# Linear attention and a gated MLP on one core: the spatial product of three batches in a 2x2 block form of seven products, denominators inverted on few columns, and another rule for the order

## The chip, the cores and the metric

The kernel runs on one core of one Trainium2 chip. The metric is the time of one execution in device microseconds (us), as the median of several runs. Less is better. Engines are called by their names in the profile: PE is TensorE (matmuls; PEld its loads of the stationary operand), DVE is VectorE, ACT is ScalarE, POOL is GpSimd, and SP (SyncE) issues nearly all DMAs.

## The reference

Linear attention over four batches of four heads (1088 positions, 32 columns a head) gives x of 1088 x 128 for each batch. It goes through an MLP whose gate mixes the positions:

```python
kv  = einsum('bhsf,bhsd->bhfd', phi(k), v)           # phi: 64 products a_i*b_j of two 8-wide projections
den = einsum('bhsf,bhf->bhs', phi(q), sum_s phi(k)) + 1e-6
x   = einsum('bhsf,bhfd->bhsd', phi(q), kv) / den    # heads side by side: (4, 1088, 128)

h    = gelu(x @ w_in)                # 128 -> 1024
u, v = h[..., :512], h[..., 512:]
v_n  = (v - mean(v)) / sqrt(var(v) + 1e-6) * g_ln
v_s  = einsum('ts,bsd->btd', w_sg, v_n) + b_sg       # w_sg: 1088 x 1088, the spatial product
out  = x + (u * v_s) @ w_out         # 512 -> 128
```

All values are fp32.

## The kernel before

**Numbers in two words.** TensorE multiplies fp32r words. Each fp32 operand is split into a high word and a low word (a cast on ACT, a subtraction on DVE), and a product takes three matmuls: high by high, low by high, high by low.

**The spatial product.** The 1088 positions that are summed over make nine row tiles t, eight of 128 rows and a last one of 64. The last needs two matmuls, since its tile holds the high words in its upper and the low words in its lower half. The 512 columns of v make four column blocks (db), the 1088 result positions three chunks (ci) of 364, 362 and 362 (376, 376 and 336 in the last batch). A unit (db, ci) is 3 matmuls into `pu` (L395 to L397, the u half of `w_in`), 26 into `pz` (L378: vh by w_h, L380: vl by w_h, L386: vh by w_l) and 3 into `po` (L463 to L465, by `w_out`). Here `w_h` and `w_l` hold the high and low words of `w_sg`, transposed, for the whole run, and `vh`, `vl` those of one column block of the normalized v (L363, L368, L371).

**Around a unit.** ACT takes `pu` through the gelu (L400). DVE moves `pz` out of its bank, scaled by `g_col` with `b_bc` added (L407), multiplies by u (L430), and with ACT's cast splits the result into `gh`, `gl` (L433, L434). After the fourth block of a chunk DVE adds x (L473, L474), and SP stores the result (L475).

**The next batch meanwhile.** While batch b is swept, attention of batch b+1 is made as side work: k projections (L189 PE, L192 ACT, L148 DVE), the sum kv (L204), q projections (L231 splits q, L237 to L239), and the features of q. These go by way of DRAM: `ab` is written to `e_0d` and its like repeated (L158, L163), read back as two operands of 128 rows (L169), multiplied (L248), and split (L250 on ACT, L251 on POOL). L261 to L263 give numerator and denominator together. ACT puts the denominators, each repeated over its head's 32 rows, into `den` (L267), DVE inverts all 128 rows (L270) and multiplies (L274), and x is split (L278, L280). Then come v (L299 to L301), gelu (L305), mean and variance, the inverse root by small operations on DVE (L320 to L345), and the normalized v (L350).

**The order.** A head, with a table of its own (`HEAD`), loads and splits the weights (the low words of w at L951) and makes attention of batch 0. Then every batch's units go in a loop, and `Plan` puts the side work between them at ticks from two tables, `FIRST` for batch 1 and `LATER` for 2 and 3. A scheduler below gives the evacuations of a unit priority (`AHEAD`). SP issues its DMAs in program order; when one waits, those behind it wait too.

## Time and profile before

| | |
|---|---|
| time, median of 3 runs (lowest, highest) | 358.16 us (357.82, 358.75) |
| span of the profiled execution, first to last instruction | 356.8 us |
| granted TensorE clock, mean | 0.997 |
| PE, DVE, ACT, POOL busy | 348.4, 233.5, 186.2, 22.1 us |
| DMA traffic | 30.19 MB, 28.1% of 16 engines' span in SP's queue |
| instructions | 5497 |

The profiled execution's own time is its span and what lies around it; the median of the three runs is 1.4 us above that span. In a group's row stand the line, engine and operation, the result and operands, shapes and count, then busy us, mean ns of one, and the idle time of the engine just ahead of the group with what ended it. A row of a timeline starts with the start and the duration in us. A row of waits has the total, the count and the longest. A row by windows gives for each stretch the busy time and count of each engine, the granted clock, the share of the DMA engines and GB/s. A DMA row ends with KB of one and the us from issue to landing.

### The profile page before, as it was taken

How to read it: one execution, taken by the hardware profiler on the slowest of the kernel's cores; microseconds unless marked ns; L12 is line 12 of the kernel's file. 1: busy time of each engine (PE TensorE's matmuls, PEld its weight loads, DVE VectorE, ACT ScalarE, POOL GpSimd, SP SyncE). 2: the span in 40 equal slices, each digit the busy share in tenths (PEclk: the TensorE clock that was granted, in tenths of full speed). 3: DMA queues.
4: the chain of work that ended last, by engine and by line, in shares of the span. 5: the costliest groups of instructions: out<-in, count | busy, mean ns of one | idle time of the engine just before them, and what ended most of it. 6: DMA issues, size and time to landing. Idle time of an engine off the chain costs nothing.

```text
span 356.8 us, 5497 instructions
## 1 busy us (share of the span) xinstructions
PE 348.4 (98%) x2024; PEld 323.1 (91%) x2024; DVE 233.5 (65%) x552; ACT 186.2 (52%) x463; POOL 22.1 (6%) x37
## 2 busy tenths in 40 slices
PE   8999999999999999999999999999999999999995
PEld 7875669898999989999898999999998999999994
DVE  4797899987929359636846766654867656552333
ACT  5475951346394983314558992323368992132120
POOL 0003000131020000022020000021120000000000
PEclk9999999999999999999999999999999999999998
DMA  7993001959200032883000006671000000100001
GB/s 228 396 410 136 2 0 31 215 153 250 71 0 2 1 83 87 224 226 121 2 0 21 3 21 147 189 177 54 0 2 1 2 0 24 42 0 2 0 2 62
DMA packets 18266, 30.19 MB, mean 85 GB/s; under 512 B 1984, under 2 KB 15168, under 8 KB 18240
## 3 DMA queue, kind: packets, MB, share of 16 engines
q1 hardware_dynamic: 18096, 29.76, 28.1%
q8 instruction: 16, 0.26, 0.3%
q10 hardware_dynamic: 144, 0.09, 0.1%
q14 instruction: 10, 0.08, 0.1%
HBM read 20.92 MB, written 8.91 MB: 84 GB/s over the span
## 4 chain that ended last, share of the span: by engine, by line
PE 88%; DVE 5%; ACT 3%; POOL 1%; issue 1%; DMA 1%; DVEq 0%; ACTq 0%
PE pz L378 19%; PE pz L386 19%; PE pz L380 17%; PE pkv L204 3%; PE pu L395 2%; PE pz L937 2%; PE po L465 2%; PE pu L397 2%; PE pu L396 2%; PE po L463 2%; PE po L464 2%; PE pv L299 2%; PE pab L813 2%; PE pk L189 2%; PE pv L300 2%; PE pv L301 2%
## 5 line engine op out<-in xcount | busy, mean ns | idle before, releaser
L378 PE MATMUL pz<-w_h,vh 128*128 128x362 f32 (+3 forms) x405 | 133.7, 332 | 0.0
L386 PE MATMUL pz<-w_l,vh 128*128 128x362 f32 (+3 forms) x405 | 129.4, 329 | 0.0
L380 PE MATMUL pz<-w_h,vl 128*128 128x364 f32 (+3 forms) x360 | 118.1, 328 | 0.0
L378 PEld LDWEIGHTS pz<-w_h,vh 128*128 128x128 f32 x405 | 75.7, 188 | 1.5 <-DVE gt L407 0.6
L386 PEld LDWEIGHTS pz<-w_l,vh 128*128 128x128 f32 x405 | 75.6, 188 | 0.3
L380 PEld LDWEIGHTS pz<-w_h,vl 128*128 128x128 f32 x360 | 67.8, 188 | 0.8
L433 ACT CAST gh<-gt 128x362 fp32r<-128x362 f32 (+3 forms) x47 | 23.1, 495 | 59.0 <-PE po L464 50.5
L407 DVE SCALAR_TENSOR_TENSOR gt<-pz,g_col,b_bc 128x362 f32<-128x362 f32 (+3 forms) x47 | 27.7, 592 | 39.9 <-PE pz L386 39.4
L434 DVE TENSOR_TENSOR gl<-gt,gh 128x362 fp32r<-128x362 f32 (+3 forms) x47 | 24.8, 531 | 15.1 <-ACT gh L433 14.9
L400 ACT ACTIVATE u<-pu 128x362 f32<-128x362 f32 (+3 forms) x48 | 22.4, 471 | 18.1 <-PE pu L397 15.4
L430 DVE TENSOR_TENSOR gt<-gt,u 128x362 f32<-128x362 f32 (+3 forms) x47 | 25.0, 532 | 8.1 <-ACT u L400 7.5
L350 ACT ACTIVATE vn<-vn,nm,rs 128x512 f32<-128x512 f32 x36 | 27.7, 811 | 4.7 <-POOL nm L684 3.9
L270 DVE RECIPROCAL den<-den 128x362 f32<-128x362 f32 (+1 forms) x9 | 21.8, 2418 | 10.0 <-ACT den L267 10.0
L368 DVE TENSOR_TENSOR vl<-vn,vh 128x384 fp32r<-128x384 f32 (+2 forms) x60 | 22.9, 420 | 7.5 <-ACT vh L363 7.3
L363 ACT CAST vh<-vn 128x384 fp32r<-128x384 f32 (+1 forms) x63 | 23.1, 420 | 3.4 <-PE pz L386 3.4
L308 ACT ACTIVATE waste<-vn,mv 128x512 bf16<-128x512 f32 x27 | 19.6, 726 | 0.3
L305 ACT ACTIVATE vn<-pv 128x512 f32<-128x512 f32 x27 | 16.0, 595 | 6.4 <-PE pv L301 6.3
L937 PE MATMUL pz<-w_f,vn 128*128 128x362 f32 (+3 forms) x54 | 18.0, 476 | 0.8 <-ACT vn L350 0.7
L395 PE MATMUL pu<-x_h,win_h 128*128 128x362 f32 (+3 forms) x48 | 16.7, 349 | 0.0
L937 PEld LDWEIGHTS pz<-w_f,vn 128*128 128x128 f32 (+1 forms) x54 | 9.8, 189 | 7.6 <-ACT vn L350 2.4
L463 PE MATMUL po<-gh,wout_h 128*128 128x362 f32 (+3 forms) x47 | 16.0, 341 | 0.0
L396 PE MATMUL pu<-x_h,win_l 128*128 128x362 f32 (+3 forms) x48 | 15.7, 328 | 0.0
(201 smaller groups left out, 530.6 us busy)
## 6 DMA issues: line engine op xcount, KB each, us to landing
w_f<-in_w SPq DMA_DIRECT2D x9, 544.0 KB, 9.8
vx<-in_v SPq DMA_DIRECT2D x8, 288.0 KB, 6.6
k<-in_k SPq DMA_DIRECT2D x3, 576.0 KB, 4.2
e_0d<-ab SPq DMA_DIRECT2D x3, 364.0 KB, 4.0
e_0d<-ab SPq DMA_DIRECT2D x6, 182.0 KB, 5.3
e_0a<-e_0d SPq DMA_DIRECT2D x3, 364.0 KB, 4.7
e_0b<-e_0d SPq DMA_DIRECT2D x3, 364.0 KB, 4.6
q<-in_q SPq DMA_DIRECT2D x6, 181.0 KB, 2.4
```

What stands on the lines that cost most here:

```text
L350: A.activation(self.vn[:, t], self.vn[:, t], AF.Identity, bias=self.nm[:, t : t + 1], scale=self.rs[:, t : t + 1])
L363: A.copy(vh[:, ts], vs[:, ts])
L378: last = mm(z, lhsT=vh[:, t], rhs=w_h[:, t, cs], start=(t == 0), stop=False)
L380: last = mm(z, lhsT=vl[:, t], rhs=w_h[:, t, cs], start=False, stop=False)
L386: mm(z, lhsT=self.parts[db][0][:, t], rhs=w_l[t][:, c0 : c0 + cw], start=False, stop=(t == NT - 1))
L395: mm(pu, lhsT=win_h[:, ws], rhs=xh[:, cs], start=True, stop=False)
L407: V.scalar_tensor_tensor(gt, z, g_col[:, db : db + 1], b_bc[:, c0 : c0 + cw], op0=ALU.mult, op1=ALU.add)
L430: V.tensor_mul(gt, gt, u)
L433: A.copy(gh, gt)
L434: V.tensor_sub(gl, gt, f32(gh))
L463: mm(o, lhsT=wout_h[:, db], rhs=gh, start=(db == 0), stop=False)
L937: return mm(zs[ci], lhsT=g.vn[r, t, :P], rhs=w_f[t][r, c0 : c0 + cw], start=(t == 0), stop=(t == NT - 1),)
```

## The change

**Seven products.** In batches 1 to 3 two column blocks (A1 = 2p, A2 = 2p + 1) are worked together. Over the result chunks 0 and 1, now of 362 columns each, and the row tiles 0 to 3 and 4 to 7, the product is a 2x2 block product. `pair` does it in seven block products of 4 row tiles x 3 matmuls, where eight were done before. Four operands are sums of blocks of v, made and split on DVE and ACT by 512 columns (`words`); four operands of w are its own blocks, and the others are sums of blocks. The last 64 rows (`tail`) and chunk 2, of 364 columns (`whole`), stay as they were. A pair has nine evacuations (`evac`, L859) instead of six: three of them add onto an earlier result, and some take the negated `ng_col`. Batch 0 keeps the plain product.

**Sums of w.** `combine` makes them once, while batch 0 is swept, from reloaded pieces of w: DVE and ACT build and split them, and SP writes them to DRAM as t1, t2, t3, beside a copy tb of the block that stood there; a fourth stays on chip (`t4a`, `t4b`). `stream` then loads one of them into columns 362 to 723 of `w_h` and `w_l`, four row tiles and two words a time, so that the same place holds another operand for the next product: streams 1, b, 2 and 3 in each pair (1 and b alone in the very last).

**Denominators.** One row of each head's denominators is written to DRAM as 4 x 364, read back as 112 x 13, inverted there (L1081), written back, and read as 128 rows, four rows repeated 32 times (L1079 to L1083); then comes the multiplication (L1084).

**Features of q.** `ab` goes to DRAM once (L1051). One operand is read with repeated rows (L1053), the other by `spread` (L792), eight loads of 16 rows.

**Smaller moves.** The subtraction that was L251 on POOL is on DVE (L1062). The small operations of the norm go from DVE to POOL. The low words of w (L739) leave the head's table and are made in the new order.

**The order.** `Plan` is now a list scheduler over all the work behind the head: each instruction has an engine, a duration, and what it reads and writes; PE's main work is in its given sequence, the side work has fractions of a batch in `SIDE`, and `DELAY` holds back the `po` matmuls.

The diff, cut to its core:

```diff
-CH = [(0, 364), (364, 362), (726, 362)]
+CH = [(0, 362), (362, 362), (724, 364)]
+CA = [(0, 364), (364, 364), (728, 360)]
+CD = [13, 13, 12]
+HW = 181
...
-FIRST = [
-    -15.472, 20.135, 12.008, 13.876, 14.942, 31.02, 18.196, 16.249, 11.271, 38.899, 15.025, 30.832, 23.931,
...
+DELAY = 5.83
+SIDE = [
+    dict(k=(0, 0.0241), q=(0.065, 0.0107), n=(0.0314, 0.1822), v=(0.6703, 0.0732)),
...
-            G.tensor_sub(qpl, a, f32(qph))
...
-            V.reciprocal(den, den)
...
+    def spread(e, d):
+        for i in range(R):
+            last = load(e[16 * i : 16 * i + 16], d)
+        return last
...
+    def group(z, zk, cw, e, t, w, wk, first, last):
+        def f():
+            o, (wh, wl) = z()[:, :cw], w()
+            mm(o, lhsT=ar[e][:, 0, t], rhs=wh, start=first, stop=False, skip_group_check=True)
+            mm(o, lhsT=ar[e][:, 1, t], rhs=wh, start=False, stop=False, skip_group_check=True)
+            mm(o, lhsT=ar[e][:, 0, t], rhs=wl, start=False, stop=last, skip_group_check=True)
...
+    def stream(n, half):
+        for t in range(4):
+            add("SP", dma(370), lambda t=t: [load(f32(w_h[:, t + half, 362:724]), td[n][t, 0]), load(f32(w_l[t + half][:, 362:724]), td[n][t, 1])],
+                r=[("td", n, t)], w=[("w", t + half, 1)])
...
+            add("SP", 0.08, lambda cw=cw, ci=ci: load(dd[ci][0, :, :cw], now["r2"][0:P:32, :cw]), r=[("r", 2, 0), ("r", 2, 1)], w=[("dd", ci)])
+            add("SP", 0.08, lambda cw=cw, ci=ci, n=n, dr=dr: load(dr, dd[ci][0, :, :cw].rearrange("h (i n) -> h i n", n=n)), r=[("dd", ci)], w=["dr"])
+            add("V", 0.5, lambda dr=dr: [V.tensor_scalar(dr, dr, EPS, None, op0=ALU.add), V.reciprocal(dr, dr)], w=["dr"])
...
+            add("SP", dma(190), lambda cw=cw, ci=ci: load(now["r4"][:, :cw], dd[ci][1, :, :cw].unsqueeze(1).broadcast_to([H, 32, cw])), r=[("dd", ci)], w=[("r", 4)])
...
+        add("V", dv(512), lambda: V.tensor_add(a[0, 0], a[0, 0], a[1, 0]), r=ak[1, 0], w=ak[0, 0])
+        add("V", dv(512), lambda: V.tensor_add(sg, a[0, 0], a[1, 1]), r=ak[0, 0] + ak[1, 1], w=gk)
+        words(ar[e[2]], lambda: sg, ("ar", e[2]), gk)
+        words(ar[e[3]], lambda: a[0, 0], ("ar", e[3]), ak[0, 0])
...
+        unit(b, ca)
+        product(X, xk, e[0], (0, 0), True)
+        evac(b, c11, X, xk, g_col)
+        whole(Z, zk, 2, e, 0)
...
+        product(X, xk, e[2], (0, 1), False)
+        stream("1", 0)
...
+        product(X, xk, e[3], (4, 1), False)
+        stream("b", 4)
...
+        product(Z, zk, e[0], (0, 1), True, (1, 1))
+        if more:
+            stream("2", 0)
...
+        product(X, xk, e[2], "t4", False, (0, 2))
...
+        product(Z, zk, e[1], (4, 1), False, (1, 3))
+        if more:
+            stream("3", 4)
```

**Where instructions stand.** First PE in the sweep of batch 1. Before, early in the sweep of a batch, two units stand side by side (`pz_0_0` and `pz_0_1` are the accumulators of block 0, chunks 0 and 1; `pu`, `po` and `pab` those of the u half, of the result and of the q projection):

```order
L397 MATMUL pu_0_1_2393<-x_l,win_h 128x362
L378 MATMUL pz_0_1_2399<-w_h,vh_0_2099 128x362
L380 MATMUL pz_0_1_2399<-w_h,vl_0_2100 128x362
L386 MATMUL pz_0_1_2399<-w_l_525,vh_0_2099 128x362
L378 MATMUL pz_0_1_2399<-w_h,vh_0_2099 128x362
L380 MATMUL pz_0_1_2399<-w_h,vl_0_2100 128x362
L386 MATMUL pz_0_1_2399<-w_l_573,vh_0_2099 128x362
L463 MATMUL po_0_1838<-gh_3_0_2214,wout_h 128x364
L237 MATMUL pab_0_2406<-qt_0h,sk_h 128x364
L378 MATMUL pz_0_0_2327<-w_h,vh_0_2099 128x364
L238 MATMUL pab_0_2406<-qt_0h,sk_l 128x364
L380 MATMUL pz_0_0_2327<-w_h,vl_0_2100 128x364
```

In the changed kernel, in the first pair of batch 1 (`w_l_636` is row tile 0 of w's low words, `t4a` the sum kept on chip, `ar_92` and `ar_94` operands of v, `bz_608` and `bz_609` the two accumulators, each with one of the seven products):

```order
L927 MATMUL bz_609<-w_h,ar_94 128x362
L928 MATMUL bz_609<-w_h,ar_94 128x362
L929 MATMUL bz_609<-w_l_636,ar_94 128x362
L881 MATMUL po_0_1817<-gh_602,wout_h 128x362
L882 MATMUL po_0_1817<-gh_602,wout_l 128x362
L883 MATMUL po_0_1817<-gl_604,wout_h 128x362
L843 MATMUL bs_607<-x_h,win_h 128x364
L844 MATMUL bs_607<-x_h,win_l 128x364
L845 MATMUL bs_607<-x_l,win_h 128x364
L927 MATMUL bz_608<-t4a,ar_92 128x362
L928 MATMUL bz_608<-t4a,ar_92 128x362
L929 MATMUL bz_608<-t4a,ar_92 128x362
```

Row tiles of two products stand interleaved: behind the first row tile of the product that reads stream 1, other units and the product by the sum on chip are put before its second row tile.

SP about the passage from batch 0 to batch 1. Before, loads for batch 2 (`in_k`, `in_v`, `in_q`) and the repetition of the features (`e_2d` of one batch, then `e_0d` of the next, from `ab`):

```order
L181 DMA k_2107<-in_k 128x1152
L169 DMA e_2b<-e_2d 128x2x362
L185 DMA vx<-in_v 128x576 x2
L225 DMA q_0_2353<-in_q 128x364
L225 DMA q_1_2359<-in_q 128x362
L225 DMA q_2_2536<-in_q 128x362
L158 DMA e_0d<-ab_0_2410 256x1x364
L163 DMA e_0d<-ab_0_2410 16x8x364 x2
```

In the changed kernel, in the first pair of batch 1 (`t_613` is t1, `t_614` and `t_615` the other two sums, `dq_618` the features on their way, x8 eight loads in a row):

```order
L996 DMA w_l_715<-t_614 128x362
L1051 DMA dq_618<-ab 64x364
L1080 DMA dr_124<-dd_620 112x13
L1039 DMA qld<-in_q 128x364
L996 DMA w_h<-t_613 128x362
L996 DMA w_l_636<-t_613 128x362
L1053 DMA e_1751<-dq_618 128x1x364
L792 DMA e_1759<-dq_618 16x364 x8
L1053 DMA e_1776<-dq_618 128x1x364
L792 DMA e_1784<-dq_618 16x364 x8
L996 DMA w_h<-t_613 128x362
L996 DMA w_l_656<-t_613 128x362
```

Between row tile 0 (`w_l_636`) and row tile 1 (`w_l_656`) of stream 1 there are 18 loads of features. In the first pair of batch 2 the same loads stand within stream b, and the way back of the denominators stands ahead of it:

```order
L1051 DMA dq_618<-ab 64x364
L1082 DMA dd_620<-dr_124 112x13
L900 DMA out<-gt_597 128x362
L996 DMA w_h<-tb 128x362
L996 DMA w_l_760<-tb 128x362
L996 DMA w_h<-tb 128x362
L996 DMA w_l_774<-tb 128x362
L1053 DMA e_2666<-dq_618 128x1x364
L792 DMA e_2673<-dq_618 16x364 x8
L1053 DMA e_2685<-dq_618 128x1x364
L792 DMA e_2690<-dq_618 16x364 x8
L996 DMA w_h<-tb 128x362
```

Here tiles 4 and 5 of b are ahead of the features and tiles 6 and 7 behind them.

More of the change, by code (lines that the diff above doesn't have):

```diff
@@ L77, in f32, with f32r @@
     return ap.bitcast(F32)
+def f32r(ap):
+    return ap.bitcast(F32R)
 class Pool:
@@ L1046, in tile_kernel @@
-    for b in range(B):
-        first, extra = (1, start()) if b == 0 else (0, [])
-        if b + 1 < B:
-            s = Side(b + 1, (NB - first) * 27)
-            with ExitStack() as stack:
-                if b == 0:
-                    for ins in head.last:
-                        stack.enter_context(tc.issue_after(ins))
-                g.main(late, s.tick, first, pend, extra)
-                s.plan.run()
-            g = s.g
-        else:
-            g.end(NB - 1, len(CH) - 1)
-            g.main(late, lambda: None, first, pend)
@@ new lines, in slot, with area @@
+    def slot(b, p):
+        return p * (1 + b % 2)
+    def area(b, db, half):
+        s, sub = slot(b, db // 2), db % 2
+        c = 256 * s + P * sub
+        if half == 2:
+            return vn[:, 8, c : c + P]
+        return vn[:, 4 * half : 4 * half + 4, c : c + P]
+    for c in range(3):
+        add(None, 0, None, w=[("po", c)], start=START["PE"])
+    for t in range(NT):
+        lo = add("V", 1.29, head.s.steps["wlo", t][2], w=[("w", t, c) for c in range(3)], after=[lo] if t else [])
@@ new lines, in tile_kernel, with pemain, unit @@
+    done_lo = lo
+    clock = [0.0]
+    def pemain(dur, f, d=0.0, **kw):
+        i = add("PE", dur, f, pos=clock[0] + d, **kw)
+        if d == 0.0:
+            clock[0] += dur
+        return i
+    nout = {}
+    def unit(b, q, d=0.0):
+        db, ci = q
+        c0, cw = CH[ci]
+        k = ("pu", b, q)
+        xh, xl = xs[b % 2]
+        def f():
+            o, cs, ws = ps(k)[:, :cw], slice(c0, c0 + cw), slice(P * db, P * db + P)
+            mm(o, lhsT=win_h[:, ws], rhs=xh[:, cs], start=True, stop=False)
+            mm(o, lhsT=win_l[:, ws], rhs=xh[:, cs], start=False, stop=False)
+            mm(o, lhsT=win_h[:, ws], rhs=xl[:, cs], start=False, stop=True)
+        pemain(3 * pe(cw), f, d, r=[("win",)] + [("x", b % 2, c) for c in range(3)], take={k: "ps"})
+        u = ("u", b, q)
+        add("A", 0.05 + ac(cw), lambda: A.activation(utt[plan.got[u]][:, :cw], ps(k)[:, :cw], AF.Gelu_apprx_tanh),
+            r=[k], take={u: "u"}, free=[k])
@@ new lines, in product @@
+    def product(z, zk, e, where, first, more=None):
+        for t in range(4):
+            if where == "t4":
+                w, wk = (lambda t=t: t4(t)), ("t4", t)
+            else:
+                w, wk = (lambda t=t: wsel(t + where[0], where[1])), ("w", t + where[0], where[1])
+            group(z, zk, HW * 2, e, t, w, wk, first and t == 0, t == 3 and more is None)
+        if more:
+            tail(z, zk, *more)
+    td = {n: dram.tile([4, 2, P, HW * 2], F32, name="t" + n) for n in ("1", "2", "3", "b")}
@@ new lines, in tile_kernel, with at, standard @@
+    dq = [dram.tile([64, CW], F32, name=f"dq{i}") for i in range(3)]
+    dd = [dram.tile([2, H, CW], F32, name=f"dd{i}") for i in range(3)]
+    def at(b, kind, i):
+        a, d = SIDE[b - 1][kind]
+        return starts[b - 1] + (a + d * i) * LONG[b - 1]
+    starts, LONG = [0.0], (104.0 - 8, 70.0, 70.0, 58.0)
+    for n in LONG:
+        starts.append(starts[-1] + n)
+    def standard(b, db, ci, zi, e, i):
+        zk = ("psn", zi)
+        unit(b, (db, ci))
+        whole(lambda: pzt[zi], zk, ci, e, i)
+        evac(b, (db, ci), lambda: pzt[zi], zk, g_col)
+        gate(b, (db, ci), DELAY)
@@ new lines, in tile_kernel @@
+    for ci in range(3):
+        evac(0, (1, ci), zs[ci], zks[ci], g_col, free=["z12"] if ci == 2 else ())
+        if ci:
+            unit(0, (1, ci))
+        gate(0, (1, ci), DELAY)
+    attention(1)
+    for ci in (0, 1, 2):
+        standard(0, 2, ci, ci % 2, (2, 3), 1)
+        if ci == 0:
+            for h in range(2):
+                split(0, 3, h, h)
+            rest(0, 3, 2)
+            combine()
+    for n, ci in enumerate((1, 0, 2)):
+        standard(0, 3, ci, (n + 1) % 2, (0, 1), 2)
+        if ci == 1:
+            stream("2", 0)
+            stream("3", 4)
@@ L1064 @@
+    zi, e = 0, (2, 3, 0, 1)
+    for b in range(1, B):
+        clock[0] = starts[b]
+        if b == B - 1:
+            before_end(b)
+        pair(b, 0, e, zi)
+        if b + 1 < B:
+            attention(b + 1)
+        pair(b, 1, e, 1 - zi)
+    with tc.manual_schedule():
+        plan.run(START, START["PE"])
 def kernel(q, k, v, S1, S2, moe_w_in, moe_g_ln, moe_w_sg, moe_b_sg, moe_w_out):
```

1019 lines of the change are left out of this document (570 added, 449 removed), and 11 rows, old and new, of tables (FIRST, LATER).

## The prediction

> **What bounds the kernel now.** I read the page first: busy times, the clock by slices, the chain of waits.
>
> ```profile
> PE 348.4 (98%) x2024; PEld 323.1 (91%) x2024; DVE 233.5 (65%) x552; ACT 186.2 (52%) x463; POOL 22.1 (6%) x37
> PEclk9999999999999999999999999999999999999998
> PE 88%; DVE 5%; ACT 3%; POOL 1%; issue 1%; DMA 1%; DVEq 0%; ACTq 0%
> ```
>
> TensorE is busy for 98% of the span at full clock, and holds 88% of the chain that ended last. A busy time of pipelined matmuls counts overlaps, so the price of one is read from the timeline, as the distance between starts. This is the first of 23 spatial matmuls in a row, and the matmul behind them:
>
> ```profile
> 199.69 0.33 PE L380 MATMUL pz<-w_h,vl 128*128 128x362 f32 x1
> ...
> 203.52 0.32 PE L463 MATMUL po<-gh,wout_h 128*128 128x362 f32 x1
> ```
>
> (203.52 − 199.69) / 23 = 0.1665 us for one matmul of 362 columns. Then the engines by stage (the head, then the sweeps of batches 0 to 3, each cut at the first unit of its batch), and who TensorE waited for:
>
> ```profile
> 0.00:51.00 51.00, 48.77 (x242) 35.11 (x242) 39.73 (x123) 33.46 (x60) 3.60 (x18) 1.00 0.55 205
> 51.00:120.00 69.00, 68.06 (x402) 64.29 (x402) 53.94 (x101) 35.05 (x97) 7.08 (x7) 1.00 0.35 93
> 120.00:204.00 84.00, 82.96 (x492) 78.79 (x492) 54.15 (x133) 49.87 (x134) 5.70 (x6) 1.00 0.30 82
> 204.00:286.00 82.00, 82.00 (x497) 79.42 (x496) 53.69 (x126) 46.68 (x125) 5.71 (x6) 1.00 0.26 64
> 286.00:357.00 71.00, 66.60 (x398) 65.50 (x396) 31.95 (x72) 21.16 (x49) 0.00 (x0) 0.98 0.05 17
> PE pk L189 <- ACT u L400: 1.1, 2, 0.8
> PE warm L144 <- POOL vx L124: 0.9, 1, 0.9
> PE pz L937 <- ACT vn L350: 0.7, 2, 0.5
> ...
> PE pnd L852 <- DVE qp L820: 0.2, 1, 0.2
> ```
>
> From 51 us on TensorE has almost no hole, and its waits, eight rows of which the first three and the last stand here, come to 4.0 us in all. So each matmul taken out counts in full, and each wait put in does too. VectorE (columns: PE, PEld, DVE, ACT, POOL, clock, DMA share, GB/s) uses 54 us of 82 to 84 in batches 1 and 2, but 54 of 69 in batch 0; the DMA engines a third or less.
>
> **Part 1, the matmuls.** A pair of column blocks took 6 x 26 = 156 spatial matmuls. Now seven products of 4 row tiles x 3 matmuls make 84, four ends of column groups on the last 64 rows 8, the two chunks left whole 52: 144. Six pairs save 72 x 0.1665 = **−12.0 us**. The order of the instructions has just these counts, so this term is sure, apart from the pitch. The Trainium skill (TensorE: Matmul & The Clock Gate, Back-to-back issue gap) gives N/2.4 + 2.5 ns for a lone warm stream, 153 ns at 362 columns, by which the saving would be 11.0 us; the trace has 166.5, and the measurement decides.
>
> **Part 2, rewriting w in place.** The product needs three sums of w's blocks beside the block itself in the same columns, so SP writes them over one another: four streams a pair of eight loads of 185 KB, 192 loads. What a DMA costs on SP and until it lands:
>
> ```profile
> 86.55 0.37 SPq L169 DMA_DIRECT2D e_2b<-e_2d  x1
> 87.02 0.41 SPq L185 DMA_DIRECT2D vx<-in_v  x1
> 87.52 0.38 SPq L225 DMA_DIRECT2D q<-in_q  x1
> out<-o SPq DMA_DIRECT2D x6, 181.0 KB, 2.2
> e_0d<-ab SPq DMA_DIRECT2D x6, 182.0 KB, 5.3
> GB/s 228 396 410 136 2 0 31 215 153 250 71 0 2 1 83 87 224 226 121 2 0 21 3 21 147 189 177 54 0 2 1 2 0 24 42 0 2 0 2 62
> ```
>
> An issue holds SP 0.37 to 0.41 us, back to back 0.47 to 0.50; I take 0.42. Landing of 181 KB is 2.2 us at best, 5.3 us when the queue is full. A stream's first load may go once the last matmul on that row tile has read, and has to land before the next product reads it. In the order of the changed kernel that leaves, over the twelve streams that are read next (streams 1 and b; 2 and 3 have over 140 matmuls of time), 33 matmuls in the first pair of batch 1 and 41 to 62 in the others: 41 x 0.1665 = 6.8 us or more. A stream alone needs 8 x 0.42 = 3.4 us of SP and 2.2 us of landing; its fourth row tile comes free 9 matmuls = 1.5 us after the first, so it takes 4.1 us, and at the best rate of the GB/s row (1.48 MB at 410 GB/s) 3.6 + 2.2 − 1.5 = 4.3 us. Hidden, with some 2.5 us to spare.
>
> Two streams are broken up on SP. In the first pair of batch 1 the loads of row tile 1 of stream 1 stand behind 18 loads of the q features (two e loads, sixteen 16-row spreads). They land 2 x 0.42 + 18 x 0.42 + 2 x 0.42 + 2.2 = 11.4 us after tile 0 came free; TensorE wants them 43 matmuls later, 7.2 us: **+4.3 us**. In the first pair of batch 2 another 18 stand within stream b; 18 x 0.42 + 4 x 0.42 + 2.2 = 11.4 us against 62 matmuls, 10.3 us: **+1 us**. Both ends: nothing, if a 23 KB issue is much cheaper than any row of this trace, and 5 us more if they land in 5.3 us. No row has a 16-row load; the nearest, a 2 KB load of g_col, held SP like the large ones, so I take 0.42.
>
> ```profile
> 13.05 0.33 SPq L839 DMA_DIRECT2D g_col<-in_g  x1
> ```
>
> The Trainium skill (DMA: Bandwidth & Descriptors, Rules for kernel authors) says to coalesce small transfers and calls those under 64 KB mostly overhead; the 144 spreads are such. Another section of that page, Issuing engines are not separate DMA queues, calls the sequencer's time to initiate a DMA usually small beside the DMA itself; by that the 5.3 us would be near nothing.
>
> **Part 3, work on VectorE and ScalarE.** What the added and removed work costs:
>
> ```profile
> L407 DVE SCALAR_TENSOR_TENSOR gt<-pz,g_col,b_bc 128x362 f32<-128x362 f32 x24 | 14.1, 593 | 16.5 <-PE pz L386 16.3
> L659 DVE TENSOR_TENSOR win_l<-wi0t,wi0e 128x512 fp32r<-128x512 f32 x1 | 0.7, 694 | 0.0
> L434 DVE TENSOR_TENSOR gl<-gt,gh 128x362 fp32r<-128x362 f32 x24 | 12.7, 530 | 1.3 <-ACT gh L433 1.2
> L270 DVE RECIPROCAL den<-den 128x362 f32<-128x362 f32 x6 | 14.5, 2416 | 8.2 <-ACT den L267 8.2
> L951 DVE TENSOR_TENSOR w_l<-w_f,w_h 128x1088 fp32r<-128x1088 f32 x8 | 10.3, 1283 | 0.0
> 107.39 0.53 DVE L434 TENSOR_TENSOR gl<-gt,gh 128x362 fp32r<-128x362 f32 x1
> 107.83 0.53 DVE L430 TENSOR_TENSOR gt<-gt,u 128x364 f32<-128x364 f32 x1
> 108.32 2.42 DVE L270 RECIPROCAL den<-den 128x362 f32<-128x362 f32 x1
> L368 DVE TENSOR_TENSOR vl<-vn,vh 128x128 fp32r<-128x128 f32 x24 | 5.9, 288 | 7.4 <-ACT vh L363 7.3
> L330 DVE TENSOR_TENSOR h<-h,ve 128x5 f32<-128x5 f32 x1 | 0.2, 168 | 0.0
> L684 POOL TENSOR_TENSOR nm<-np,rs 128x3 f32<-128x3 f32 x1 | 0.7, 659 | 0.1
> ```
>
> A swept batch gains 6 evacuations (3.6 us), 8 sums of 512 at 0.69 and 4 of 128 at 0.29 (6.7), 4 x 2 more splits of 512 less the narrower ones that go (some 5), 6 subtractions taken over from POOL (3.2); it loses three wide reciprocals for narrow ones (−6), half of the multiplications by them (−1.6) and some 24 small operations of the norm at 0.17, now POOL's (−4). Net some +7 on 54 us of some 78: TensorE covers it, and loses it only where VectorE is late for a bank. The norm's chain on POOL is slower by up to 0.5 us an operation (its dearest row is 0.66 for 0.17), some 2 us a group of rows; behind it stands v of the next batch, which has the rest of the batch to come, so nothing. Batch 0 is tighter. To its 53.9 us in 69 the sums of w add 8 rounds of seven operations, one of 362 columns at 0.53 and six of 181 at an estimated 0.35 (between the rows of 128 and 362), 21 us, and the nine low words of w (1.28 each) come here from the head, 11.6 us; with the reciprocals, the norm and POOL's subtractions as above (−8.5) about 78. But successive operations start closer than they last (107.39, 107.83, 108.32: 0.44 and 0.49 us for 0.53, a factor of 0.87), so the true need is about 68 of 69 us. That is full: TensorE will be held up somewhat, between 0 and 78 − 69 = 9 us. I take **+1.5 us** here, near the lower end, since the distances bear on it more than the durations. The head only loses work by this, and TensorE's waits in it are among the 4.0 us of part 5. The three extra evacuations a pair come in TensorE's shadow, since two accumulators alternate.
>
> **Part 4, the reciprocals by way of DRAM.** The nearest rows to the narrow pair of operations are those of batch 0's own denominators:
>
> ```profile
> L862 DVE TENSOR_SCALAR den<-pnd x3: 160/170/170, 17.4 to 32.1; 128x12 f32<-128x12 f32 x3
> L865 DVE RECIPROCAL den<-den x3: 228/228/228, 17.6 to 32.3; 128x12 f32<-128x12 f32 x3
> ```
>
> Per chunk 2.42 us of VectorE becomes 0.4 us, with four DMAs after one another around it. At 2.2 us landing and 0.42 us of issue the chain is about 11 us long, 8 us longer than before. It is covered for the first two chunks of each batch, whose x is wanted only when the third is there. Third chunk of batch 1: SP has 197 DMAs to issue by then, 197 x 0.42 = 83 us, in the 97 us between the last load of the head and the end of batch 0's sweep:
>
> ```profile
> 23.14 0.42 SPq L225 DMA_DIRECT2D q<-in_q  x1
> ```
>
> With waits for landings in between, the chain ends about when the last v products are due: between 0 and 5 us late, I take **+2.5 us**. For batches 2 and 3 the v products lie further back, and I cost it at nothing.
>
> **Part 5, the order.** A list puts each engine's instructions in order; it may win back part of the 4.0 us of waits quoted: between 0 and 4.0, I take **−2 us**.
>
> **Sum.** −12.0 + 5.3 + 1.5 + 2.5 − 2.0 = −4.7: 356.8 − 4.7 = 352.1 us of span. The median of the three runs, 358.16, lies 1.4 above that profiled span; so 353.5 us. A difference under 0.3%, 1.1 us, could not be told from none.
>
> **Rivals.** (A) The waits put in are all covered, since TensorE is late at those places anyway or small loads issue faster, and the order wins back all 4.0 us: −12.0 − 4.0, 340.8 + 1.4 = 342.2 us. For it: 2.5 us to spare in ten of twelve streams. Against: every issue in the trace holds SP 0.33 us or more.
>
> (B) SP becomes the bound. It issues 526 DMAs instead of 99, 526 x 0.42 = 221 us of 350, in order, and a DMA that waits (for a denominator from VectorE, for ab from ScalarE) holds back the stream behind it. Each of the other ten tight streams, 1 us late, gives −4.7 + 10 = +5.3: 362.1 + 1.4 = 363.5 us, slower. It decides from 0.5 us each, the margin of the sum over ten. For it: SP's spare time of 2.5 us is no longer than one landing of 5.3 instead of 2.2, and the waits of a denominator stand ahead of stream b in batch 2. Against: between streams SP has 15 us or more.
>
> (C) Batch 0's added work is late: VectorE needs its 78 us of durations in 69, not its 68 of distances, and the chain of part 4 comes at the end of that. Then 9 + 2.5 us stand in place of 1.5 + 2.5: −4.7 + 7.5 = +2.8, 359.6 + 1.4 = 361.0 us. For it: the sums of w read pieces that SP has to load first, and SP has its own 83 us. Against: in the windows no stage has VectorE late for TensorE by more than tenths.
>
> **How the numbers follow.** Forecast 0.50, A 0.22, B 0.13, C 0.10, and 0.05 for a case between, within 1.1 us of the time before. Forecast and A are faster: 0.72; same 0.05; B and C slower: 0.23. The likeliest case has 348 to 357 us of its own (its waits of 9.3 us more or less by some 4). The range goes from A's 342 to 363: C is in it, half of A and half of B lie outside, 0.17.
>
> **What would show it.** In the changed profile the spatial matmuls keep 0.166 us between starts, and 72 are gone. TensorE waits for a DMA on w once in the first pair of batch 1 (4 us) and briefly in the first of batch 2; waits for VectorE near the end of batch 0 show part 3, one before the v products of batch 1 part 4. If TensorE waits for w in most pairs, B is right; if TensorE waits 8 us or more for VectorE or for v before batch 1's first pair, C. If no wait on w is over 1 us, the 0.42 us for a small load was wrong.

## The result, and the profile after

The changed kernel takes 435.08 us (median of 4 runs, 433.13 to 437.52), the kernel before 358.01: a ratio of 1.215, 95% interval 1.210 to 1.219. The prediction had 353.5 us, at most 363. The profiled execution took 435.59 us, with a span of 433.8. Its page, busy times, clock, and the chain by engine and by line:

```profile
PE 365.0 (84%) x1952; PEld 335.1 (77%) x1952; DVE 265.2 (61%) x619; ACT 216.4 (50%) x517; POOL 22.7 (5%) x85
PEclk9999997979699998896958999899698899999999
PE 31%; DMA 24%; SPq 16%; DVE 12%; ACT 9%; issue 5%; POOL 3%; DVEq 0%; POOLq 0%; ACTq 0%
SPq L792 12%; DMA r<-dd 7%; PE bz L927 5%; PE bz L929 5%; PE bz L928 5%; DMA tmp<-in_w 4%; DMA dq<-ab 3%; DMA dd<-dr 3%; ACT vn L340 2%; DMA w_h<-t 2%; ACT kp L1113 2%; PE pz L725 2%; PE pab L601 2%; ACT vn L1110 2%; SPq L1053 1%
```

TensorE held 88% of the chain before and holds 31% now. DMAs and SP's queue have 40%, and the one line with most of it is L792, the eight-fold load of the q features. No engine is full any more: TensorE is busy for 84%, VectorE for 61%. The granted clock, 9 all along before, drops to 5 to 8 in many slices. The same windows as before, cut at the first unit of each batch:

```profile
0.00:58.40 58.40, 54.90 (x287) 41.90 (x288) 46.86 (x136) 35.70 (x71) 2.85 (x18) 1.00 0.55 194
58.40:167.20 108.80, 78.63 (x420) 72.62 (x418) 61.55 (x152) 49.30 (x139) 7.12 (x23) 0.89 0.52 139
167.20:277.20 110.00, 93.24 (x479) 87.67 (x480) 62.19 (x138) 61.12 (x149) 6.35 (x22) 0.86 0.61 176
277.20:366.70 89.50, 75.92 (x407) 72.56 (x406) 50.83 (x111) 46.67 (x113) 3.38 (x13) 0.92 0.58 165
366.70:434.00 67.30, 62.32 (x365) 60.31 (x364) 43.81 (x86) 23.66 (x46) 3.04 (x10) 0.99 0.47 150
```

Batch 0's sweep takes 108.8 us for 69, batch 1's 110.0 for 84, batch 2's 89.5 for 82. The last batch, which has no attention of a next one beside it, takes 67.3 for 71: there the change gains what it should. (The head seems longer since 47 more matmuls stand ahead of the cut.)

To see where the 77 us lie, each matmul of both traces is priced at the distance between starts that its width has where nothing waits (the median in the trace of before: 0.1665 us for 362 and 364 columns, 0.172 for 376, 0.154 for 336, 0.233 for 512, 0.32 for the 384 of the head's q projections, 0.11 for 128 and less). What a distance has beyond that is a hole if it is over 0.4 us, and a small delay otherwise.

| | before | changed |
|---|---|---|
| matmuls at their own distances, us | 331.2 | 319.1 |
| holes | 4.2 | 69.9 |
| small delays | 16.4 | 40.1 |
| ahead of the first and behind the last matmul | 5.0 | 4.7 |
| span | 356.8 | 433.8 |

The matmuls became 12.1 us cheaper, as forecast. Holes of 66 us and small delays of 24 us came in. TensorE's own waits, four rows of them, are mostly for VectorE, and for w there is one:

```profile
PE po L883 <- DVE gl L874: 12.7, 2, 6.9
PE bs L1014 <- DVE kp L268: 8.0, 5, 5.3
PE bs L1071 <- DVE e L1062: 7.8, 4, 3.9
...
PE bz L927 <- DMA w_h<-t: 3.8, 1, 3.8
```

Here is one hole from its origin on, in batch 0: first SP, then VectorE, then TensorE (start, duration, and in brackets the idle time ahead and its releaser).

```profile
101.48 8.55 SPq L792 DMA_DIRECT2D e<-dq  x16
110.08 0.94 SPq L973 DMA_DIRECT2D tmp<-in_w  x2
```

```profile
103.58 0.53 DVE L874 TENSOR_TENSOR gl<-gt,gh 128x364 fp32r<-128x364 f32 x1
112.69 0.35 DVE L978 TENSOR_TENSOR tmp<-tmp 128x181 f32<-128x181 f32 x1 [8.58 <-DMA tmp<-in_w]
112.99 0.53 DVE L1060 TENSOR_TENSOR e<-e,e 128x360 f32<-128x360 f32 x1
113.44 0.34 DVE L979 TENSOR_TENSOR tmp<-tmp 128x181 f32<-128x181 f32 x1
113.70 0.53 DVE L874 TENSOR_TENSOR gl<-gt,gh 128x362 fp32r<-128x362 f32 x1
```

```profile
108.19 0.32 PE L882 MATMUL po<-gh,wout_l 128*128 128x362 f32 x1
114.28 0.67 PE L883 MATMUL po<-gl,wout_h 128*128 128x362 f32 x1 [5.77 <-DVE gl L874]
114.75 0.51 PE L927 MATMUL bz<-w_h,ar 128*128 128x364 f32 x1
115.05 0.50 PE L928 MATMUL bz<-w_h,ar 128*128 128x364 f32 x1
115.36 0.51 PE L929 MATMUL bz<-w_l,ar 128*128 128x364 f32 x1
```

SP spends 8.55 us on sixteen spread loads. The two loads of pieces of w behind them go out only at 110.08. VectorE stands at the sum that reads them for 8.58 us, and behind that sum stands `gl`, which has nothing to do with w. TensorE waits for `gl` for 5.77 us. When it goes on, its matmuls start 0.30 us apart instead of 0.1665, at a granted clock of 0.50 (112.5 to 119 us): it runs at half rate. VectorE and TensorE stand in line behind SP's queue. VectorE's waits, and the issues of L792, say that this is no single case:

```profile
DVE e L1060 <- DMA e<-dq: 38.4, 13, 5.9
DVE r L1084 <- DMA r<-dd: 26.9, 8, 6.3
DVE gt L859 <- PE bz L939: 18.8, 13, 4.1
DVE gl L874 <- ACT gh L873: 17.2, 16, 3.5
DVE tmp L978 <- DMA tmp<-in_w: 16.9, 5, 8.6
```

```profile
L792 SPq DMA_DIRECT2D e<-dq x144: 303/418/1490, 56.2 to 323.4; - x144
```

82 us of VectorE's waits are for three kinds of DMA: features, inverted denominators, pieces of w. The way of one chunk's denominators, in the chain of waits during batch 1's sweep (start, us):

```profile
229.20 4.42 DMA dd<-r
233.63 2.21 DMA dr<-dd
236.33 2.04 DMA dd<-dr
238.42 5.41 DMA r<-dd
243.86 0.55 DVE r L1084
```

From the first issue to the multiplication 14.7 us pass, where a wide reciprocal took 2.42.

### The profile page after: what moved, and what is told of

The parts are those of the page before. It is cut to its first block, busy times and chain, and to the rows that moved or that the text cites. A ratio compares the mean times of both kernels' runs of the same rounds, so it can differ in the third digit from the quotient of the medians.

```text
span 433.8 us, 6285 instructions
## 1 busy us (share of the span) xinstructions
PE 365.0 (84%) x1952; PEld 335.1 (77%) x1952; DVE 265.2 (61%) x619; ACT 216.4 (50%) x517; POOL 22.7 (5%) x85
## 4 chain that ended last, share of the span: by engine, by line
PE 31%; DMA 24%; SPq 16%; DVE 12%; ACT 9%; issue 5%; POOL 3%; DVEq 0%; POOLq 0%; ACTq 0%
SPq L792 12%; DMA r<-dd 7%; PE bz L927 5%; PE bz L929 5%; PE bz L928 5%; DMA tmp<-in_w 4%; DMA dq<-ab 3%; DMA dd<-dr 3%; ACT vn L340 2%; DMA w_h<-t 2%; ACT kp L1113 2%; PE pz L725 2%; PE pab L601 2%; ACT vn L1110 2%; SPq L1053 1%
## 5 line engine op out<-in xcount | busy, mean ns | idle before, releaser
L927 PE MATMUL bz<-w_h,ar 128*128 128x362 f32 (+1 forms) x288 | 100.5, 349 | 6.0 <-DMA w_h<-t 3.8
L928 PE MATMUL bz<-w_h,ar 128*128 128x362 f32 (+1 forms) x288 | 98.8, 343 | 0.4 <-DVE ar L905 0.4
L929 PE MATMUL bz<-w_l,ar 128*128 128x362 f32 (+1 forms) x288 | 98.8, 343 | 0.0
L927 PEld LDWEIGHTS bz<-w_h,ar 128*128 128x128 f32 x288 | 58.4, 203 | 8.0 <-DMA w_h<-t 4.3
L928 PEld LDWEIGHTS bz<-w_h,ar 128*128 128x128 f32 x288 | 58.0, 201 | 1.4 <-DVE ar L905 0.6
L929 PEld LDWEIGHTS bz<-w_l,ar 128*128 128x128 f32 x288 | 57.6, 200 | 0.2 <-DMA w_l<-t 0.2
L874 DVE TENSOR_TENSOR gl<-gt,gh 128x362 fp32r<-128x362 f32 (+1 forms) x47 | 25.1, 533 | 17.3 <-ACT gh L873 17.2
L873 ACT CAST gh<-gt 128x362 fp32r<-128x362 f32 (+1 forms) x47 | 23.2, 493 | 23.9 <-DVE gt L872 22.9
L340 ACT ACTIVATE vn<-vn,st 128x512 f32<-128x512 f32 x36 | 27.9, 811 | 9.9 <-POOL st L332 5.8
L904 ACT CAST ar<-vn 128x512 fp32r<-128x512 f32 x40 | 24.7, 617 | 13.3 <-PE bz L929 12.9
L905 DVE TENSOR_TENSOR ar<-vn,ar 128x512 fp32r<-128x512 f32 x40 | 27.4, 684 | 3.8 <-ACT ar L904 3.4
L872 DVE TENSOR_TENSOR gt<-gt,u 128x362 f32<-128x362 f32 (+1 forms) x47 | 25.0, 532 | 1.5 <-ACT u L849 0.9
L859 DVE SCALAR_TENSOR_TENSOR gt<-bz,g_col,b_bc 128x362 f32<-128x362 f32 (+1 forms) x31 | 18.3, 591 | 9.3 <-PE bz L939 5.1
L1084 DVE TENSOR_TENSOR r<-r,r 128x364 f32<-128x364 f32 (+1 forms) x9 | 4.8, 537 | 26.9 <-DMA r<-dd 26.9
```

The lines of the kernel that those rows point to most:

```text
L340: A.activation(self.vn(t), self.vn(t), AF.Identity, bias=self.nm[:, t : t + 1], scale=self.rs[:, t : t + 1])
L872: add("V", dv(cw), lambda: V.tensor_mul(gt(k)[:, :cw], gt(k)[:, :cw], utt[plan.got[u]][:, :cw]), r=[u], w=[k], free=[u])
L873: add("A", ac(cw), lambda: A.copy(ght[plan.got[h]][:, :cw], gt(k)[:, :cw]), r=[k], take={h: "gh"})
L874: add("V", dv(cw), lambda: V.tensor_sub(glt[plan.got[l]][:, :cw], gt(k)[:, :cw], f32(ght[plan.got[h]][:, :cw])), r=[h, k], take={l: "gl"}, ...
L904: add("A", ac(n), lambda: A.copy(dst[:, 0], q()), r=r, w=[key])
L905: add("V", dv(n), lambda: V.tensor_sub(dst[:, 1], q(), f32(dst[:, 0])), r=r, w=[key])
```

## The experiments

Four theories stood at first. S: SP's in-order queue is the bound, above all by the 144 small loads. L: the latency of the chains through DRAM. W: the seven products themselves, with streams and sums of w. O: the list-scheduled order is worse whatever SP does.

### One load a spread operand

```diff
-        for i in range(R):
-            last = load(e[16 * i : 16 * i + 16], d)
-        return last
+        return load(e, d.unsqueeze(0).broadcast_to([R, *d.shape]))
```

> One edit: each spread operand of the q features comes by one load of 128 rows (the 16 rows repeated by the source's pattern) instead of eight loads of 16 rows. The order of all other instructions is unchanged. Theory S (SP's in-order queue is the bound: 144 issues of 0.47 us, 68 us, hold back VectorE's features and all that is queued behind them): 126 issues go, 59 us of SP; the time falls by 40 us or more, to 395 or less, and SP has no stretch of 3.8 us under one line. Theory L (the chains through DRAM, above all the denominators' four hops, are the bound): the features' loads fall off the chain but the hops stay; 415 to 425. Theory W (the seven products with their streams and sums of w are what costs): 425 or more.

Measured 394.3 us (ratio to before 1.100, 1.093 to 1.107): 41 us less by 126 issues less, with every other instruction in its place. Holes fall from 69.9 to 45.2 us. VectorE's waits for features fall by half, and those for pieces of w by a third, though no load of pieces of w was touched:

```profile
DVE r L1082 <- DMA r<-dd: 23.1, 8, 6.2
DVE e L1058 <- DMA e<-dq: 19.5, 12, 3.5
DVE gl L872 <- ACT gh L871: 16.9, 15, 3.7
DVE gt L857 <- PE bz L937: 14.9, 11, 2.9
DVE tmp L976 <- DMA tmp<-in_w: 10.9, 5, 4.2
```

As S had it (395 or less).

### The same, with the issues put back

```diff
+        last = load(e, d.unsqueeze(0).broadcast_to([R, *d.shape]))
+        for i in range(R - 1):
+            turn["scr"] = (turn.get("scr", -1) + 1) % 56
+            load(scr[:, turn["scr"] : turn["scr"] + 1], identd[:16, :1])
+        return last
```

> As the kernel with one load a spread operand, in the same order, but behind each such load stand seven loads of 64 bytes (16 rows of one number) into a corner that nobody reads. The features land as early as there; SP has as many issues as the changed kernel, 526. If the issues on SP are what costs (theory S): back to 425 to 435. If it was the landing of the last of eight pieces that the features waited for (theory L3): it stays at 390 to 400.

Measured 438.2 us, 3 us above the range of S and far from that of L3. Seven loads of 64 bytes cost as much as seven of 23 KB. SP's row for them, and TensorE's for the whole, read like those of the changed kernel:

```profile
L796 SPq DMA_DIRECT2D scr<-in_ident x126: 310/418/1508, 56.5 to 324.2; - x126
```

```profile
PE 366.0 (84%) x1952; PEld 336.8 (77%) x1952; DVE 265.5 (61%) x619; ACT 217.1 (50%) x517; POOL 22.1 (5%) x85
```

So it is the issue on SP that costs, 0.42 us for 64 bytes as for 23 KB, and neither the bytes nor the landing of the last piece.

### Denominators inverted in place

```diff
-            add("SP", 0.08, lambda cw=cw, ci=ci: load(dd[ci][0, :, :cw], now["r2"][0:P:32, :cw]), r=[("r", 2, 0), ("r", 2, 1)], w=[("dd", ci)])
...
-            add("V", 0.5, lambda dr=dr: [V.tensor_scalar(dr, dr, EPS, None, op0=ALU.add), V.reciprocal(dr, dr)], w=["dr"])
...
+            add("V", dv(cw) + 2.4, lambda cw=cw: [V.tensor_scalar(now["r2"][:, :cw], now["r2"][:, :cw], EPS, None, op0=ALU.add), V.reciprocal(now["r2"][:, :cw], now["r2"][:, :cw])], w=[("r", 2, 0), ("r", 2, 1)])
```

> One edit: the denominators are inverted where they stand, on 128 rows, by one addition and one wide reciprocal on VectorE; the four loads and stores by way of DRAM go (36 DMAs). Theory S: 36 issues of some 0.5 us and SP's waits for landings ahead of other loads, about 18 + 20 us of SP's time, part of it on the path: 405 to 420. Theory L: the 15 us chain of a chunk becomes 3 us, nine times, and TensorE's waits for x and v go: 395 or less. Theory W: 425 or more.

Measured 415.6 us (ratio 1.159, 1.155 to 1.164), 19.5 less. S's range; L alone was to give 40 us or more. Nine wide reciprocals put 9 x (2.42 − 0.40) = 18 us of work back on VectorE, and the kernel gains all the same. How much of the 19.5 us is the 36 issues and how much the chain's own length, this run does not tell.

### Without the streams

```diff
     def stream(n, half):
-        for t in range(4):
-            add("SP", dma(370), lambda t=t: [load(f32(w_h[:, t + half, 362:724]), td[n][t, 0]), load(f32(w_l[t + half][:, 362:724]), td[n][t, 1])],
-                r=[("td", n, t)], w=[("w", t + half, 1)])
+        return
```

> Leaves out the rewriting of w: the streams are not loaded, so seven of the products use the block that stands in w (the sums of w are still built and stored). 192 loads of 185 KB go, 35.6 MB and some 80 us of SP's issues. Theory W with the streams at fault: 375 or less. Theory S: SP loses 80 us of issues, but those stand mostly where SP has time; the spreads and the chain stay where they hold VectorE: 400 to 420, and batch 0's stage keeps its 109 us. Theory L: 425 or more.

Measured 417.8 us. Half of all traffic goes, and only 17 us with it. Batch 0's sweep still takes 104.6 us. S's range (400 to 420); W with the streams at fault falls.

### The plain product, all else as changed

```diff
-            combine()
...
-            stream("2", 0)
-            stream("3", 4)
...
-        pair(b, 0, e, zi)
+        plain(b, 0)
...
-        pair(b, 1, e, 1 - zi)
+        plain(b, 1)
```

`plain` splits v as batch 0 does and runs its `standard` units of 26 matmuls; the planner is given longer batches for it.

> Batches 1 to 3 use the plain product (eight block products, six units of 26 matmuls a pair), with neither sums of v and w nor streams; list-scheduled order, spreads, and denominators by way of DRAM stay. TensorE has 72 matmuls more, 12.0 us. Theory W: the loss goes with the product, 355 to 370. Theory S: batch 0 loses 88 DMAs of the sums, but each batch keeps its 54 feature loads and the hops on SP, which still hold VectorE: 385 to 410. Theory L: 405 or more.

Measured 413.4 us (ratio 1.153, 1.150 to 1.157). With its 72 matmuls back and neither sums nor streams, the kernel is still 55 us slower than before. Most of the loss is thus not the seven products' but that of the other parts: features, denominators, order. W falls as the main cause. But S had 385 to 410 and is missed by 3 us, while L's 405 or more is met; between these two the run does not decide, and its instructions stand in an order of their own.

### Nothing but other costs in the planner

```diff
-    dma = lambda kb: max(0.08, kb / 330.0)
+    dma = lambda kb: max(0.45, kb / 330.0)
...
-                add("SP", dma(200), lambda cw=cw, ci=ci, p=p: spread(
+                add("SP", 3.9, lambda cw=cw, ci=ci, p=p: spread(
```

(and 0.45 instead of 0.08 for the small loads of the denominators)

> The changed kernel with nothing but other costs given to the planner: 3.9 us for eight spread loads instead of 0.6, at least 0.45 us for any DMA instead of 0.08. All instructions are the same, in another order. Theory S1 (SP's capacity is the bound): the same issues on the same queue, 420 or more. Theory S2 (the order was made with SP's time far too cheap, and VectorE and TensorE stand in order behind loads that come late): 405 or less.

Measured 402.2 us (ratio 1.122, 1.120 to 1.125): the same instructions in another order, 33 us less. S2, then: the planner counted 0.6 us for eight loads that hold SP for 3.8, and 0.08 for a small load, and put VectorE's and TensorE's instructions where data would have been by that count. Which of the two prices weighs more was not tried. The kernel is still 44 us slower than before; this run does not tell by what.

### Both edits, features and denominators

```diff
+        return load(e, d.unsqueeze(0).broadcast_to([R, *d.shape]))
...
+            add("V", dv(cw), lambda cw=cw: V.tensor_mul(now["r3"][:, :cw], now["r3"][:, :cw], now["r2"][:, :cw]), r=[("r", 2, 0), ("r", 2, 1)], w=[("r", 3, 0), ("r", 3, 1)])
```

> Both edits that helped, together: one load a spread operand, and denominators inverted in place. 162 DMAs of the 526 go. Theory S (SP's in-order queue): the two gains (41 and 20 us) add, since each takes issues and waits off the same queue: 370 to 380, and the granted clock comes back to 0.98 or more. Theory L2 (what is left is the loads' own latency and the streams, so the second edit finds its gain already taken): 385 to 394.

Measured 375.9 us (ratio 1.050, 1.045 to 1.055): 41 and 19.5 add up to 60.5, 59.2 were found. L2 falls. The granted clock came back to 0.974 to 0.984 in the four runs, three of them short of the 0.98 that S expected.

### The plain product with both edits

```diff
-        pair(b, 0, e, zi)
+        plain(b, 0)
...
+        return load(e, d.unsqueeze(0).broadcast_to([R, *d.shape]))
```

(and the denominators as above)

> Plain product in batches 1 to 3 (no sums, no streams, 72 matmuls more), with one load a spread operand and denominators inverted in place: the new order alone, nearly. Theory S: the product's own DMAs no longer load SP, 352 to 365, about the time before. Theory O (the list-scheduled order itself is worse, whatever SP does, since it puts attention of the next batch where TensorE waits for it): 375 or more. Against the kernel with both edits and seven products it shows what the seven products gain or lose once SP is relieved: TensorE's own saving of 12.0 us would make this one 12 us slower than that one.

Measured 362.9 us (ratio 1.013, 1.010 to 1.017). O falls. But with SP relieved the seven products are 13 us slower than the plain product, though their matmuls are 12 us cheaper: 25 us of other costs come with them.

### The streams issued by POOL

```diff
-            add("SP", dma(370), lambda t=t: [load(f32(w_h[:, t + half, 362:724]), td[n][t, 0]), load(f32(w_l[t + half][:, 362:724]), td[n][t, 1])],
+            add("G", 2.0, lambda t=t: [G.dma_start(f32(w_h[:, t + half, 362:724]), td[n][t, 0]), G.dma_start(f32(w_l[t + half][:, 362:724]), td[n][t, 1])],
```

(with both edits)

> As the kernel with one load a spread operand and denominators inverted in place, and the streams of w are issued by POOL instead of SP, as tasks of POOL in the order. Theory S: 192 issues and 42 us of waits for TensorE leave SP, so feature loads, loads of pieces of w and stores pass freely: 350 to 362. Theory B (the streams' 35.6 MB on the shared DMA engines are what delays the rest): no better than with SP, 370 or more; POOL's own issue time could then make it worse.

Measured 404.0 us, against 375.9 with SP. This speaks against S in its simple form: 192 issues fewer on SP, and worse. The order changed as well, and POOL's small operations of the norm now stand behind streams that wait for TensorE; which of the two does it was not taken apart, and B is not shown by it.

### Both edits, the planner told the costs

```diff
-    LATE = dict(PE=0.25, V=0.15, A=0.18, G=0.2, SP=2.0)
+    LATE = dict(PE=0.25, V=0.15, A=0.18, G=0.2, SP=2.5)
...
-    dma = lambda kb: max(0.08, kb / 330.0)
+    dma = lambda kb: max(0.45, kb / 330.0)
```

The two stores of a sum of w are also priced at 1.0 us, and the landing of `ab` in DRAM at 3.0. The second kernel is the same with the plain product.

> One load a spread operand and denominators inverted in place (375.9 us), with the planner's costs for DMAs raised to what the traces show (at least 0.45 us of SP, 2.5 us to land, 1.0 for two stores). If the rest of its waits come from an order made with SP too cheap: 360 to 368. If they come from the sums of w and the streams themselves: 372 to 380.

> The same costs given to the planner of the kernel with the plain product (362.9 us). It has holes of 11 us on TensorE against 4 of the kernel before, 5.4 of them in batch 0. If the order there was made with SP too cheap: 355 to 360, and then it stands level with the kernel before. If not: 362 to 364.

Measured 373.5 us (ratio 1.042, 1.037 to 1.046) and 357.9 (1.001, 0.998 to 1.003). With the plain product the new order stands level with the old one. With the seven products the raised prices give only 2.4 us, and the time lies in the second range, that of the sums and streams. One long hole is left, at the first seven-product pair of batch 1:

```profile
PE bz L925 <- ACT ar L902: 13.1, 1, 13.1
```

The split waits for a sum of v, and the sum for its buffer `tmp`, which it shares with the sums of w: in the chain of waits the last of their stores lands, and then the sum is made (163.17).

```profile
160.67 2.42 DMA t<-tmp
163.17 0.70 DVE tmp L1143
```

### Without the sums of w

```diff
-            add("SP", dma(370), lambda t=t: [load(f32(w_h[:, t + half, 362:724]), td[n][t, 0]), load(f32(w_l[t + half][:, 362:724]), td[n][t, 1])],
+            add("SP", dma(370), lambda t=t: [load(f32(w_h[:, t + half, 362:724]), td["b"][t, 0]), load(f32(w_l[t + half][:, 362:724]), td["b"][t, 1])],
...
-                w, wk = (lambda t=t: t4(t)), ("t4", t)
+                w, wk = (lambda t=t: wsel(t, 0)), ("w", t, 0)
```

(both edits; `combine` keeps only the copy tb)

> Leaves out the sums of w: the kernel with one load a spread operand and denominators inverted in place, where the streams load the stored block again and again and the product by the sum on chip uses a block of w. TensorE's work, the sums of v, the evacuations and the 192 stream loads stay; in batch 0 VectorE loses 56 operations, ScalarE 24, SP 64 DMAs. If the sums are why batch 0 is 11 us longer than with the plain product and batch 1 8 us: 355 to 360. If the streams and the sums of v cost it: 368 or more.

Its four runs lie at 358.1 and between 363.6 and 365.6 us; the profile is that of 358.1, at a clock of 1.00. All of them are 10 us or more below the 375.9 with the sums. Batch 0 falls from 85.6 to 74.9 us, batch 1 from 92.9 to 84.4, batches 2 and 3 by 1.4 together. So the sums of w are the larger part of what the seven products lose by, and they lose it in batches 0 and 1. They are not all of it: with 12 us of matmuls less than the plain product's 362.9, this kernel should stand at 351, and it is 7 us or more above that. What of the sums costs it, their DMAs, their operations on VectorE and ScalarE, or their buffer, was not taken apart, since the run leaves out all three.

### A buffer of its own for the sum of v

```diff
-    NG, NU, NH, NL = 5, 3, 2, 2
+    NG, NU, NH, NL = 4, 3, 2, 2
...
+    tmp2 = gp.tile([P, 512], F32, tag="tmp2", name="tmp2")
...
-        sg = tmp[:, :512].rearrange("p (t d) -> p t d", d=P)
+        sg = tmp2[:, :512].rearrange("p (t d) -> p t d", d=P)
```

(on the 373.5 us kernel)

> The kernel with one load a spread operand, denominators inverted in place and raised costs (373.5 us), with a buffer of its own for the sum of v, which shares one with the sums of w there; one evacuation buffer of five is given up for the space. If the 13.4 us hole ahead of batch 1's first pair is the wait for that buffer (its release by the last store of a sum of w): 358 to 364. If it only moves to the next wait, since the sums are late themselves: 368 or more.

Measured 378.8 us, in the second range. The 13 us hole is gone, and others came:

```profile
PE bz L926 <- DMA w_h<-t: 8.4, 2, 4.4
PE bz L926 <- DVE gt L858: 6.0, 3, 5.2
```

The two waits for `t`, at 157.5 and 163.0 us, are in the same pair: TensorE now waits for the sums themselves, whose last store goes out at 163.1. Batch 1 gains 2 us by the buffer (95.9 for 98.0), so the buffer was only the last of several things that are late. In the 373.5 us kernel the sums are worked on from 64.7 to 161.7 us, while batch 0's sweep ends at 133.7: in this order a batch is too short for them. The wait of 5.2 us is another matter. It stands in batch 2, where no sum of w is made, and batch 2 takes 79.3 us for 71.7, more than the whole kernel lost. VectorE waits there for the store of an evacuated buffer, 3.1 us. This speaks for the second half of the edit, four evacuation buffers in place of five, but no run here has one half without the other.

### Seven products in batches 2 and 3 only

```diff
     for b in range(1, B):
...
+        if b == 1:
+            plain(b, 0)
+            attention(b + 1)
+            combine()
+            plain(b, 1)
+            continue
         pair(b, 0, e, zi)
```

(with both edits and the planner's costs; then the same with the own buffer)

> Seven products in batches 2 and 3 only: batch 1 has the plain product, and the sums of w may be built any time in batches 0 and 1. One load a spread operand, denominators inverted in place, the raised costs for DMAs. TensorE does 48 matmuls less than the plain kernel with the same costs (357.9 us), 8.0 us. Theory D (the seven products pay once their sums are not in the way of a first pair): batch 0 and 1 as with the plain product, 73 and 84 to 86 us, batches 2 and 3 as measured with them, 71.7 and 65.8: 350 to 355. Theory E (the sums cost VectorE and SP the same wherever they stand, or their buffer holds up the first pair here too): 358 or more.

> Both: seven products in batches 2 and 3 only, and the sum of v in a buffer of its own, with four evacuation buffers. Theory D: level with the kernel before it or 1 to 3 us less, 349 to 355. If four evacuation buffers are too few: more than without.

Measured 352.5 us (ratio 0.984, 0.981 to 0.988) and 351.9 (0.981, 0.978 to 0.984): both are some 6 us faster than the kernel before, under 2% but clear of the noise, and the first here to be so; the two cannot be told apart. The windows of the first:

```profile
0.00:58.20 58.20, 54.66 (x289) 41.66 (x289) 46.64 (x136) 35.90 (x72) 2.87 (x18) 1.00 0.56 194
58.20:130.00 71.80, 69.67 (x425) 67.16 (x425) 61.16 (x124) 46.60 (x125) 6.09 (x23) 1.00 0.42 122
130.00:213.50 83.50, 81.79 (x502) 80.29 (x501) 61.91 (x139) 59.38 (x153) 5.66 (x22) 1.00 0.49 140
213.50:283.50 70.00, 69.77 (x404) 67.39 (x403) 58.00 (x114) 46.46 (x114) 3.77 (x14) 1.00 0.72 217
283.50:350.00 66.50, 61.67 (x365) 60.38 (x363) 43.34 (x85) 23.68 (x46) 2.66 (x9) 0.98 0.48 151
```

Theory D: the sums are now worked on from 98.3 to 215.1 us, over much of both batches, and these take 71.8 and 83.5 us against 72.7 and 84.0 with the plain product, so the sums cost TensorE nothing. In batches 2 and 3, with all their streams (DMA engines busy for 72% of batch 2), the seven products gain 6.8 us of the 8.0 that their matmuls save; by the medians of the runs (352.5 against 357.9) it is 5.4. The sweeps side by side, in us:

| | head | batch 0 | 1 | 2 | 3 |
|---|---|---|---|---|---|
| before | 51.0 | 69.3 | 84.0 | 81.6 | 70.9 |
| changed | 58.4 | 108.7 | 110.1 | 89.5 | 67.1 |
| one load | 58.0 | 93.8 | 93.4 | 81.5 | 66.8 |
| both edits | 58.2 | 85.6 | 92.9 | 74.2 | 66.3 |
| both, told costs | 57.6 | 76.1 | 98.0 | 71.7 | 65.8 |
| plain, both, told costs | 57.9 | 72.7 | 84.0 | 73.2 | 70.0 |
| seven products late | 58.2 | 71.8 | 83.5 | 70.0 | 66.4 |

## Why the prediction was wrong

**Part 1 was right.** −12.0 us forecast; the matmuls of the trace are 12.1 us cheaper, at 0.1665 us.

**Part 2 had the right price and charged it at the wrong place; this is the step that failed.** A 16-row load was priced at 0.42 us of SP: the median is 0.418. But it was charged only in the two places where features stand ahead of a stream, +5.3 us, because the sum asked of each load only when TensorE needs the data. TensorE did wait for w once in the first pair of batch 1, 3.8 us for a forecast 4.3. What was missed are the other neighbours of the 144 loads: VectorE stands in order at the features and at pieces of w, and its evacuations, splits and products stand behind them. So the loads that were put at 5.3 us cost 41: the two edits to `spread` show it (41 us less, and 44 more with the issues put back).

**Part 4 had the mechanism and an eighth of the size.** The chain was put at 11 us, hidden but for 2.5; the one shown is 14.7 us long, since its first and last hops take 4.4 and 5.4 for 2.2, and taking the chains out gave 19.5, issues included. "Covered for the first two chunks" overlooked the same thing as part 2: VectorE waits for the chain in order, 26.9 us in all. Part 2 had read 5.3 us in a row of before, and put it down to a full queue. But at 129.1 us of that trace the first of those repeated stores lands in 5.0 us with nothing moving ahead of it (0 GB/s from 128 to 129).

**Part 5 had the wrong sign.** The order was to win back 2 us of 4.0. Made with 0.6 us for eight loads and 0.08 for a small one, it lost 33, by the run with nothing but other costs. The prediction had seen SP's true price, and that the order is a list built on durations, but did not set the two beside each other. These 33 us and the 41 and 19.5 of the two edits are largely the same time: with both edits made, raising the prices gave 2.4 us more with the seven products and 5.0 with the plain product. Late loads did the harm, and much of it goes with either, with the loads themselves or with an order that knows of them.

**Part 3 and rival C.** By the letter of its sign C came, since TensorE waits for VectorE for more than 8 us. But VectorE was never full: 61.6 us busy in batch 0's 108.8. It stood idle at instructions that wait for DMAs, so neither the durations nor the distances of its work set the time. The sums of w did cost batch 0 and what follows: 76.1 us against 72.7 with the plain product, both with the raised prices, and the 13 us hole behind them.

**Rival B** named SP's queue with waits at its head, but put the price into tight streams, 10 us, where most of it lies in the features and hops. By its sign, waits for w in most pairs, it did not come: without all streams 17 of 77 us go.

**Half rate behind holes was not thought of.** 24 of the 77 us are small delays, and 20 of these 24 lie on matmuls that take 1.6 to 2.2 times their own distance, in stretches like the one at 114.75, where starts are 0.30 us apart. A long hole is thus paid for a second time. The full clock of the rows of before was taken as given for after.

**What stays open.** The terms above overlap and don't add up to 77 us. Of the 25 us that come with the seven products once SP has fewer issues, 7 or more are not the sums of w, and no run took them apart.

## What to carry to other kernels

When a change adds DMAs, count their issues on the queue that makes them, and then ask of every engine, not of the bottleneck alone, what stands behind each instruction that waits for such a load: one in-order engine with an early wait hands it on to all. A planner's cost table is part of the kernel: check each price in it against a trace, the number of issues in a task above all, before its order is trusted. A saving with a one-time cost (here the sums of w) may only pay if that cost has idle time to lie in; here the kernel that gave up the saving in one batch of three was the faster one.
